# The last head's output weights on 16 partitions, in a load of two times 8

## Chip, cores, metric

The kernel runs on one core of one Trainium2 chip. The metric is the device time of one execution in microseconds (us). Three runs of the kernel before took 1311.43, 1311.44 and 1311.72 us; the median is 1311.44.

## What is computed

One decoding step of a block with grouped-query attention and a gate. There are 2 batch rows, 32 query heads over 8 key/value heads, 32768 cached positions, head size 128, model size 512, all in float32. Cut to what matters:

```
xn  = layernorm(x)                                  # (2, 1, 512)
q   = xn @ wq                                       # 32 heads of 128
s   = softmax(q k^T / sqrt(128)) v                  # per head, 32768 keys and values
att = concat(s) @ wo                                # wo is (4096, 512)
g   = silu(relu(xn @ w1 + b1)^2 @ w2 + b2)
out = x + att * g
```

The caches are 2 x 8 x 32768 x 128 numbers each, 537 MB together; wq and wo are 8.4 MB each.

## The kernel before

**Stages.** The work goes over 16 pairs s of a key/value head and a batch row (`hkv, b = divmod(s, 2)`). For each, the keys come in four quarters: VectorE transposes them in 32 x 32 blocks (L248), TensorE makes the scores with q as the stationary side (L253), a softmax follows (`softmax`, `probs`), and TensorE sums the values with the probabilities (L316, `values`). When a pair's values are summed, its four heads are turned into columns of `oT` (L323 to L328). After the last pair the output projection runs (`project`, L395 to L404), the result is multiplied by the gate and added to x (L406, L407), and two small stores end the kernel (L409).

**Transfers.** Nearly all loads are issued by SP, in the order of the list `loads` (L136 to L141). An entry with an event is issued when that event is given (`give`), and waits on SP until its buffer has been read. Keys go to three slots of 4 MB (`kslots`), values to `vbuf` of 8 MB; the value load before the last goes to the first two key slots. The output weights come last: `load_wo(i)`, i = 0 to 3, each a group of 8 heads or 1024 rows of wo, 2 MB. Groups 0 and 1 lie in slot 2, groups 2 and 3 in slot 0, which is free when TensorE has read the first half of the value load before the last.

**The layout of wo.** A group is loaded as `(p j) e -> p j e`: partition p holds the eight rows 8p to 8p+7 of the group, 16 KB without a break. For the projection, row 8p+j must meet the attention output of the same number, so the columns of `oT` (partition = place in the head, one column per head) are spread to `oW[p, i, j, b]`. That happens when the second head pair of a group is done (`hkv % 2 == 1`, L329 to L336): VectorE multiplies the 8 columns by the selector `sele` (L332), TensorE multiplies that by `selj` (L335), ScalarE copies the 8 columns (L336). `project` then makes one matmul for each j and each of 4 column groups of 128 outputs; `oW` has 32 columns for the batch, of which 2 are used. A float32 matmul stands in the profile as two instructions.

**The last group** comes in four pieces of j (`PIECES`, L33, L128, L129): 4, 2, 1 and 1 of the eight rows of every partition, that is 1 MB, 512 KB and twice 256 KB. The projection takes groups 0, 1, 2 and then the pieces in this order.

The order of instructions on an engine is made by the framework's scheduler from the program's order; waits between engines are semaphores that it sets.

Of the kernel before, what the change touches and what calls it, by code (L numbers as in the profile page):

```python
# [9 lines left out]
F32 = mybir.dt.float32  # L10
AF = mybir.ActivationFunctionType
ALU = mybir.AluOpType
AX = mybir.AxisListType

P = 128
# [14 lines left out]
TS = (1, 0, 2, 3)  # L30
NT = 4
HALF = 64 * 128
PIECES = ((0, 4), (4, 6), (6, 7), (7, 8))  # L33


@with_exitstack
def gqa_decode_kernel(ctx: ExitStack, tc: tile.TileContext, x, kc, vc, wq, wo, w1, b1, w2, b2, out):
    nc = tc.nc
    B, _, D = x.shape
    _, HKV, SK, DH = kc.shape  # L40
    HQ = wq.shape[1] // DH
# [7 lines left out]
    DE = D // NG  # L49
    WG = 8  # L50
    NWG = HQ // WG
# [6 lines left out]
    const = ctx.enter_context(tc.tile_pool(name="const", bufs=1))  # L58
    ktpool = ctx.enter_context(tc.tile_pool(name="ktpool", bufs=8))
    work = ctx.enter_context(tc.tile_pool(name="work", bufs=2))  # L60
# [3 lines left out]
    def misc(name):  # L64
        return pms.tile([P, 512], F32, tag="ms", name=name)
# [51 lines left out]
        return t.rearrange("p (j e) -> p j e", j=FJ)  # L117


    def load_wo(i):  # L120
        if i % 2 == 0:
            wide[i // 2] = kslots[:, 2 - i].rearrange("p (i j e) -> p i j e", i=2, j=WG)
        t = wide[i // 2][:, i % 2]
        src = wo[i * WG * P:(i + 1) * WG * P, :].rearrange("(p j) e -> p j e", p=P)
        if i < NWG - 1:
            nc.sync.dma_start(t, src)
        else:
            for j0, j1 in PIECES:  # L128
                nc.sync.dma_start(t[:, j0:j1, :], src[:, j0:j1, :])  # L129
        return t  # L130

    wide = {}
    NK, NV = NS * NT, NS * NCH
    kslots = const.tile([P, 3, HALF], F32, name="kslots")
    vbuf = const.tile([P, 2 * HALF], F32, name="vbuf")
    loads = [(None, load_wq, 0), (None, load_half, 0), (None, load_half, 1), (("q", 0), load_w1, 0),  # L136
             (("s", 0), load_half, 2), (None, load_half, 3), (("q", 0), load_w2, 0)]
    for m in range(2, NV):
        loads += [(("s", 2 * m - 2), load_k, m), (("v", m - 3) if m > 2 else ("w", 1), load_v, m - 2)]
    loads += [(("s", NK - 2), load_v, NV - 2), (("v", NV - 3), load_v, NV - 1)]  # L140
    loads += [(("s", NK - 1), load_wo, 0), (("s", NK - 1), load_wo, 1), (("v", NV - 2), load_wo, 2), (("v", NV - 2), load_wo, 3)]  # L141
    past = {None}
    done = [0]
# [7 lines left out]
    def take(f, a):  # L151
        return tiles.pop((f, a))

    def give(*event):
        past.add(event)
        issue()
# [4 lines left out]
    ident = const.tile([P, P], F32, name="ident")  # L161
# [12 lines left out]
    selj = const.tile([P, WG], F32, name="selj")  # L174
    nc.vector.tensor_reduce(selj, ident.rearrange("p (e j) -> p j e", j=WG), axis=AX.X, op=ALU.add)
    sele = const.tile([P, P // WG], F32, name="sele")
    nc.vector.tensor_reduce(sele, ident.rearrange("p (e j) -> p e j", j=WG), axis=AX.X, op=ALU.add)
    oT = const.tile([P, HQ, B], F32, name="oT")
    oW = const.tile([P, NWG, WG, 32], F32, name="oW")
    nc.gpsimd.memset(oW, 0.0)  # L180
    sc = [pone.tile([P, 512], F32, tag=f"sc{i}", name=f"sc{i}") for i in range(NT)]
    o_ps = [pone.tile([P, 512], F32, tag=f"o{i}", name=f"o_ps{i}") for i in range(2)]
    for t in o_ps:
# [16 lines left out]
    t_ps = misc("xnT_ps")  # L200
# [6 lines left out]
    for d in range(ND):  # L207
        for f in range(2):
            for g in range(NG):
                cc = f * NG + g  # L210
                nc.tensor.matmul(sc[f][32 * g:32 * g + 32, :], xnT[:, d, 0:32], wqt[:, d, cc * 512:(cc + 1) * 512],  # L211
                                 start=(d == 0), stop=(d == ND - 1))
    give("q", 0)
    qT = const.tile([P, B, HKV, REP, 4], F32, name="qT")
    for f in range(2):
        for h in range(REP):
# [3 lines left out]
            t_ps = misc(f"qT_ps{f}_{h}")  # L220
# [87 lines left out]
    def values(n):  # L308
        s, k = divmod(n, NCH)
        vt = take(load_v, n)  # L310
        o = o_ps[s % 2]
        for c in range(2):
            for i in range(NO // 4):
                for g in range(NG):
                    lo = (c * NG + g) * NO + 4 * i
                    nc.tensor.matmul(o[32 * g:32 * g + 16, :], pT[s][:, k, g, c, 4 * i:4 * i + 4, :].rearrange("p o h -> p (o h)"),  # L316
                                     vt[:, lo:lo + 4, :].rearrange("p o d -> p (o d)"),
                                     start=(k + c + i == 0), stop=(k == NCH - 1 and c == 1 and i == NO // 4 - 1))
        give("v", n)
        if k == NCH - 1:  # L320
            hkv, b = divmod(s, B)
            o_sb = work.tile([P, 512], F32, tag="o_sb", bufs=1, name=f"o_sb{s}")
            nc.scalar.copy(o_sb, o)  # L323
            t_ps = misc(f"oT_ps{s}")
            r4 = rs.pop(s)
            for i in range(4):
                nc.tensor.matmul(t_ps[:, :REP], o_sb[:, i * DH:(i + 1) * DH], r4[:, i, :], start=(i == 0), stop=(i == 3))  # L327
            nc.vector.tensor_copy(oT[:, hkv * REP:(hkv + 1) * REP, b], t_ps[:, :REP])  # L328
            if hkv % 2 == 1:  # L329
                i = hkv // 2  # L330
                m = work.tile([P, WG, P // WG], F32, tag="om", bufs=1, name=f"om{s}")
                nc.vector.tensor_mul(m, oT[:, i * WG:(i + 1) * WG, b:b + 1].to_broadcast([P, WG, P // WG]),  # L332
                                     sele[:, None, :].to_broadcast([P, WG, P // WG]))
                t_ps = misc(f"oW_ps{s}")
                nc.tensor.matmul(t_ps[:, :WG], m.rearrange("p h e -> p (h e)"), selj, start=True, stop=True)  # L335
                nc.scalar.copy(oW[:, i, :, b], t_ps[:, :WG])  # L336


    hT, gate = first[:, 3, :FJ * 32].rearrange("p (j b) -> p j b", j=FJ), const.tile([P, DE], F32, name="gate")
# [33 lines left out]
    for n in range(NK):  # L373
        s, i = divmod(n, NT)
        if i == 0:
            set_q(s)
        scores(n)
        if n == 1:
            mlp_up()
        if n == 3:  # L380
            mlp_down()
        if i == 3:
            softmax(s)
        if n >= 5 and n % 2 == 1:
            values((n - 5) // 2)
        if i == 3:
            probs(s)
    values(NV - 2)
    values(NV - 1)


    a_ps = sc[0]
    wot = [take(load_wo, i) for i in range(NWG)]

    def project(i, j0, j1):  # L395
        for j in range(j0, j1):
            for g in range(NG):
                nc.tensor.matmul(a_ps[32 * g:32 * g + 32, :DE], oW[:, i, j, :], wot[i][:, j, g * DE:(g + 1) * DE],
                                 start=(i == 0 and j == 0), stop=(i == NWG - 1 and j == WG - 1))

    for i in range(NWG - 1):
        project(i, 0, WG)
    for j0, j1 in PIECES:
        project(NWG - 1, j0, j1)  # L404
    asb = work.tile([P, DE], F32, tag="e", bufs=1, name="a_sb")
    nc.vector.tensor_mul(asb, gate, a_ps[:, :DE])  # L406
    nc.vector.tensor_add(xe, asb, xe)  # L407
# [25 lines left out]
```

## Time and profile before

| what | before |
|---|---|
| time, median of 3 runs | 1311.44 us |
| the profiled execution, its own time | 1311.62 us |
| its span, first to last instruction | 1309.6 us |
| TensorE matmul (PE), weight load (PEld) busy | 885.4, 251.1 us |
| VectorE (DVE), ScalarE (ACT), GpSimd (POOL) busy | 648.8, 88.3, 15.1 us |
| moved by DMA | 561.74 MB, mean 429 GB/s |
| packets of queue q1 (SP's), of q8 (instructions) | 10952, 38 |

The profile is of one execution. Busy times are shares of the span in which an engine worked; DMA share is the mean busy share of the core's 16 DMA engines, PEclk the granted clock of TensorE, 1.00 being full speed. A line of the timeline gives start, duration, engine, line of the kernel, operation, tiles and count; brackets hold the idle time before it and what ended that. The trace also holds one record for each DMA packet (start, duration, size, queue) and one for each completion mark. A load that uses 16 DMA engines ends with 16 marks; who waits for the load waits for all of them.

### The profile page before, as it was taken

Reading aid. Unit: us, or ns where it says so; the run is one execution under the profiler, and the core shown is the slowest. Engines: PE = TensorE matmul, PEld = TensorE weight load, DVE = VectorE, ACT = ScalarE, POOL = GpSimd, SP = SyncE. Lnnn points to the kernel's source line nnn. Section 1 sums busy time; section 2 is a strip of 40 time slices with the busy share of each in tenths; the row PEclk is TensorE's granted clock in tenths of the full one; section 3 lists DMA queues with packets and bytes.
Section 4 is the critical chain, followed back from the end, with each engine's and each line's share of the span. In section 5 each row is a group of like instructions: output and inputs, shape, how many; then the busy total and the mean of one; then the engine's idle time right before and its main releaser. Section 6 shows DMA issues by size and latency. Waiting matters only on the chain.

```text
span 1309.6 us, 11506 instructions
## 1 busy us (share of the span) xinstructions
PE 885.4 (68%) x4926; PEld 251.1 (19%) x4926; DVE 648.8 (50%) x742; ACT 88.3 (7%) x237; POOL 15.1 (1%) x76
## 2 busy tenths in 40 slices
PE   3867675658757567775657766566875756776575
PEld 1222121112212111121212211111221211112123
DVE  2855654435555344655435565443655534465410
ACT  0010010101001010000101001010000101000010
POOL 0000000000000000000000000000000000000000
PEclk9988877888878788877789978778987878888788
DMA  9999999999999999999999999999999999999997
GB/s 403 433 441 439 424 439 423 441 433 431 435 427 435 435 427 443 423 439 428 437 429 431 435 427 443 419 443 429 435 435 427 439 427 437 435 425 441 421 441 303
DMA packets 11040, 561.74 MB, mean 429 GB/s; under 512 B 1239, under 2 KB 1259, under 8 KB 1646
## 3 DMA queue, kind: packets, MB, share of 16 engines
q1 hardware_dynamic: 10952, 561.00, 99.2%
q8 instruction: 38, 0.62, 0.2%
q14 instruction: 12, 0.10, 0.0%
q10 hardware_dynamic: 38, 0.02, 0.0%
HBM read 561.01 MB, written 0.00 MB: 428 GB/s over the span
## 4 chain that ended last, share of the span: by engine, by line
DMA 74%; DVE 18%; issue 5%; PE 2%; SPq 0%; DVEq 0%
DMA kslots<-in_A_k_cache 68%; DVE kt L248 18%; DMA kslots<-in_A_wo 2%; DMA kslots<-in_A_v_cache 2%; DMA vbuf<-in_A_wq 2%; PE sc L211 1%; PE o_ps L316 0%; PE h_ps L347 0%; SPq L129 0%; DVE qr L218 0%; DVEq L248 0%; PE qT_ps L222 0%; PE sc L253 0%; DVE h L354 0%; DVE first L355 0%
## 5 line engine op out<-in xcount | busy, mean ns | idle before, releaser
L253 PE MATMUL sc<-kt,qz 128*32 128x512 f32 x2048 | 578.4, 671 | 330.6 <-DVE kt L248 309.0
L248 DVE STREAM_TRANSPOSE kt<-kslots 128x1024 f32<-128x1024 f32 x512 | 580.7, 1205 | 350.9 <-DMA kslots<-in_A_k_cache 350.9
L253 PEld LDWEIGHTS sc<-kt,qz 128*32 128x32 f32 x2048 | 112.0, 115 | 783.1 <-DVE kt L248 580.7
L316 PE MATMUL o_ps<-vbuf,pT 128*16 128x512 f32 x1984 | 228.8, 597 | 11.0 <-DMA vbuf<-in_A_v_cache 11.0
L316 PEld LDWEIGHTS o_ps<-vbuf,pT 128*16 128x16 f32 x1984 | 76.7, 97 | 139.9 <-issue 119.6
L275 ACT ACTIVATE p<-sc,nm 128x512 f32<-128x512 f32 x32 | 23.3, 746 | 991.0 <-DVE nm L271 991.0
L328 DVE COPY oT<-oT_ps 128x4 f32<-128x4 f32 x16 | 2.6, 162 | 121.5 <-PE oT_ps L327 121.5
L258 DVE TENSOR_REDUCE rm<-sc 128x1 f32<-128x512 f32 x32 | 22.1, 691 | 63.9 <-PE sc L253 63.9
L294 ACT COPY pT<-pT_ps 64x256 f32<-64x256 f32 x128 | 46.8, 366 | 19.7 <-PE pT_ps L290 18.2
L300 DVE RECIPROCAL r<-l_ps 128x4 f32<-128x4 f32 x16 | 2.9, 182 | 46.2 <-PE l_ps L298 46.2
L231 POOL COPY qz<-qT 32x16 f32<-32x16 f32 x64 | 12.7, 198 | 1077.4 <-PE sc L253 1042.5
L327 PE MATMUL oT_ps<-rs,o_sb 128*128 128x4 f32 x128 | 16.9, 255 | 11.5 <-ACT o_sb L323 11.4
L290 PE MATMUL pT_ps<-ident,p 128*128 128x128 f32 x128 | 20.2, 309 | 2.9 <-ACT p L275 2.9
L327 PEld LDWEIGHTS oT_ps<-rs,o_sb 128*128 128x128 f32 x128 | 15.5, 191 | 25.6 <-ACT o_sb L323 25.6
L298 PE MATMUL l_ps<-lh,ones 128*128 128x4 f32 x32 | 8.2, 327 | 17.6 <-ACT pT L294 17.6
L290 PEld LDWEIGHTS pT_ps<-ident,p 128*128 128x128 f32 x128 | 17.4, 169 | 3.1 <-ACT p L275 3.1
L323 ACT COPY o_sb<-o_ps 128x512 f32<-128x512 f32 x16 | 9.4, 585 | 100.1 <-PE o_ps L316 100.1
L278 DVE TENSOR_REDUCE l<-l 128x1 f32<-128x2 f32 x16 | 2.5, 155 | 26.9 <-ACT p L275 26.9
L264 PE MATMUL mx_ps<-ident,rm 128*128 128x128 f32 x16 | 5.2, 323 | 14.6 <-DVE rm L262 14.6
L202 PE MATMUL xnT_ps<-ident,xn 128*128 128x128 f32 x4 | 1.1, 428 | 20.4 <-DVE xn L198 20.4
L316 PE MATMUL o_ps<-kslots,pT 128*16 128x512 f32 x64 | 8.4, 682 | 4.2 <-DMA kslots<-in_A_v_cache 4.2
L298 PEld LDWEIGHTS l_ps<-lh,ones 128*128 128x128 f32 x32 | 6.8, 266 | 22.0 <-ACT pT L294 22.0
(68 smaller groups left out, 116.2 us busy)
## 6 DMA issues: line engine op xcount, KB each, us to landing
kslots<-in_A_k_cache SPq DMA_DIRECT2D x4, 4096.0 KB, 20.8
vbuf<-in_B_w SPq DMA_DIRECT2D x2, 3584.0 KB
kslots<-in_A_wo SPq DMA_DIRECT2D x3, 2048.0 KB
kslots<-in_A_wo SPq DMA_DIRECT2D x1, 1024.0 KB
kslots<-in_A_wo SPq DMA_DIRECT2D x1, 512.0 KB
kslots<-in_A_wo SPq DMA_DIRECT2D x2, 256.0 KB, 31.3
vbuf<-in_A_v_cache SPq DMA_DIRECT2D x31, 31.0
kslots<-in_A_k_cache SPq DMA_DIRECT2D x30
```

Source lines behind the costliest of these rows:

```text
L211: nc.tensor.matmul(sc[f][32 * g:32 * g + 32, :], xnT[:, d, 0:32], wqt[:, d, cc * 512:(cc + 1) * 512], start=(d == 0), stop=(d == ND - 1))
L231: nc.gpsimd.tensor_copy(qz[s % 2][32 * a:32 * a + 32, 16:].rearrange("p (e y) -> p e y", e=4)[:, :, a * REP:(a + 1) * REP], qT[32 * a:32 * ...
L248: nc.vector.transpose(r.rearrange("p e o w -> p o e w"), kt[:, g * NO:(g + 1) * NO, e0 * 32:(e0 + 2) * 32].rearrange("p o (e w) -> p o e w ...
L253: nc.tensor.matmul(bank[32 * g:32 * g + 32, :], qz[s % 2][:, lo + 32 * (e0 + e):lo + 32 * (e0 + e) + 32], kts[g][:, e].rearrange("p o w -> ...
L258: nc.vector.tensor_reduce(rm[s][:, u:u + 1], bank, axis=AX.X, op=ALU.max)
L275: nc.scalar.activation(p[:, :, :, u], sc[2 * (s % 2) + u].rearrange("p (o w) -> p o w", w=32), AF.Exp, bias=nm, scale=SCALE, accum_out=l2[ ...
L290: nc.tensor.transpose(t_ps[:, j * P:(j + 1) * P], p[:, o:o + 2].rearrange("p o w u -> p (o w u)"), ident)
L294: nc.scalar.copy(sb[64 * a:64 * a + 64].rearrange("p k g c (i j o) h -> p i o j (g c) k h", i=2, o=2)[:, i, o], v[:, :, :, :, a])
L298: nc.tensor.matmul(t_ps[:, :REP], ones, lh, start=True, stop=True)
L316: nc.tensor.matmul(o[32 * g:32 * g + 16, :], pT[s][:, k, g, c, 4 * i:4 * i + 4, :].rearrange("p o h -> p (o h)"), vt[:, lo:lo + 4, :].rear ...
L323: nc.scalar.copy(o_sb, o)
L327: nc.tensor.matmul(t_ps[:, :REP], o_sb[:, i * DH:(i + 1) * DH], r4[:, i, :], start=(i == 0), stop=(i == 3))
```

## The change

The last group is no longer one block of 1024 rows. Its last head (128 rows of wo, 256 KB) is loaded by itself to 16 partitions (`few`, in slot 1), 8 rows or 16 KB on each. The source is written `(n y j) e -> y n (j e)` with y = 2, so that partition 8y+n holds the rows 8(2n+y) to 8(2n+y)+7 of the head. This load is issued ahead of the others. The seven heads before it come in three pieces of 4, 2 and 1 heads; each piece is now a block of its own (`(p j) e -> p j e` with j = 4, 2, 1), where a partition's rows lie together in wo.

The spread to `oW` changes accordingly for this group: one multiply and matmul for the four heads, one for the two, a copy for the single head, and one for the last head into `oF`, 16 partitions by 8 rows. Two selector pairs (`sels`) are made at the start. `oW` has 16 batch columns instead of 32. The projection takes groups 0 to 2, then the four heads, the eight rows of `few`, the two heads and the one.

```diff
-PIECES = ((0, 4), (4, 6), (6, 7), (7, 8))
+PIECES = ((0, 4, 0), (4, 2, 4), (6, 1, 6))
...
-            for j0, j1 in PIECES:
-                nc.sync.dma_start(t[:, j0:j1, :], src[:, j0:j1, :])
+            base = (HQ - 1) * P
+            nc.sync.dma_start(few, wo[base:base + P, :].rearrange("(n y j) e -> y n (j e)", y=2, j=WG))
+            for h0, nh, j0 in PIECES:
+                base = (i * WG + h0) * P
+                nc.sync.dma_start(t[:, j0:j0 + nh, :], wo[base:base + nh * P, :].rearrange("(p j) e -> p j e", p=P))
...
+few = kslots[0:16, 1, 0:WG * D]
...
+    for nh in (4, 2):
+        sels[nh] = const.tile([P, P // nh + nh], F32, name=f"sel_{nh}")
+        nc.vector.tensor_reduce(sels[nh][:, 0:P // nh], ident.rearrange("p (e j) -> p e j", j=nh), axis=AX.X, op=ALU.add)
+        nc.vector.tensor_reduce(sels[nh][:, P // nh:], ident.rearrange("p (e j) -> p j e", j=nh), axis=AX.X, op=ALU.add)
-    oW = const.tile([P, NWG, WG, 32], F32, name="oW")
+    oW = const.tile([P, NWG, WG, 16], F32, name="oW")
+    oF = const.tile([16, WG, 16], F32, name="oF")
...
+                def spread(h0, nh, se, sj, x0):
+                    m = work.tile([P, P], F32, tag="om", bufs=1, name=f"om{s}_{h0}")
+                    nc.vector.tensor_mul(m.rearrange("p (h e) -> p h e", h=nh),
+                                         oT[:, h0:h0 + nh, b:b + 1].to_broadcast([P, nh, P // nh]),
+                                         se[:, None, :].to_broadcast([P, nh, P // nh]))
+                    nc.tensor.matmul(t_ps[:, x0:x0 + nh], m, sj, start=True, stop=True)
...
+                    for h0, nh, j0 in PIECES[:-1]:
+                        spread(i * WG + h0, nh, sels[nh][:, 0:P // nh], sels[nh][:, P // nh:], j0)
+                    h0, _, x0 = PIECES[-1]
+                    nc.scalar.copy(oW[:, i, 0:x0, b], t_ps[:, :x0])
+                    nc.vector.tensor_copy(oW[:, i, x0, b:b + 1], oT[:, i * WG + h0, b:b + 1])
+                    m = work.tile([P, P], F32, tag="om", bufs=1, name=f"om{s}_few")
+                    nc.vector.tensor_mul(m[:, 0:16].rearrange("p (y n) -> p y n", y=2),
+                                         oT[:, HQ - 1:HQ, b:b + 1].to_broadcast([P, 2, 8]),
+                                         sele.rearrange("p (n y) -> p y n", y=2))
+                    nc.tensor.matmul(t_ps[0:16, 8:8 + WG], m[:, 0:16], selj, start=True, stop=True)
+                    nc.scalar.copy(oF[:, :, b], t_ps[0:16, 8:8 + WG])
...
-    for j0, j1 in PIECES:
-        project(NWG - 1, j0, j1)
+    project(oW[:, NWG - 1], wot[NWG - 1], j0, j0 + nh)
+    project(oF, few.rearrange("p (j e) -> p j e", j=WG), 0, WG)
+    for h0, nh, j0 in PIECES[1:]:
+        project(oW[:, NWG - 1], wot[NWG - 1], j0, j0 + nh, stop=(j0 + nh == WG - 1))
```

More of the change, by code (lines that the diff above doesn't have):

```diff
@@ L177, in gqa_decode_kernel @@
     nc.vector.tensor_reduce(sele, ident.rearrange("p (e j) -> p e j", j=WG), axis=AX.X, op=ALU.add)
+    sels = {}
+    for nh in (4, 2):
+        sels[nh] = const.tile([P, P // nh + nh], F32, name=f"sel_{nh}")
+        nc.vector.tensor_reduce(sels[nh][:, 0:P // nh], ident.rearrange("p (e j) -> p e j", j=nh), axis=AX.X, op=ALU.add)
+        nc.vector.tensor_reduce(sels[nh][:, P // nh:], ident.rearrange("p (e j) -> p j e", j=nh), axis=AX.X, op=ALU.add)
     oT = const.tile([P, HQ, B], F32, name="oT")
-    oW = const.tile([P, NWG, WG, 32], F32, name="oW")
+    oW = const.tile([P, NWG, WG, 16], F32, name="oW")
     nc.gpsimd.memset(oW, 0.0)
+    oF = const.tile([16, WG, 16], F32, name="oF")
+    nc.gpsimd.memset(oF, 0.0)
     sc = [pone.tile([P, 512], F32, tag=f"sc{i}", name=f"sc{i}") for i in range(NT)]
@@ L330, in values @@
                 i = hkv // 2
-                m = work.tile([P, WG, P // WG], F32, tag="om", bufs=1, name=f"om{s}")
-                nc.vector.tensor_mul(m, oT[:, i * WG:(i + 1) * WG, b:b + 1].to_broadcast([P, WG, P // WG]),
-                                     sele[:, None, :].to_broadcast([P, WG, P // WG]))
                 t_ps = misc(f"oW_ps{s}")
-                nc.tensor.matmul(t_ps[:, :WG], m.rearrange("p h e -> p (h e)"), selj, start=True, stop=True)
-                nc.scalar.copy(oW[:, i, :, b], t_ps[:, :WG])
+                def spread(h0, nh, se, sj, x0):
[4 more added lines that the diff above has]
+                    nc.tensor.matmul(t_ps[:, x0:x0 + nh], m, sj, start=True, stop=True)
+                if i < NWG - 1:
+                    spread(i * WG, WG, sele, selj, 0)
+                    nc.scalar.copy(oW[:, i, :, b], t_ps[:, :WG])
+                else:
+                    for h0, nh, j0 in PIECES[:-1]:
[9 more added lines that the diff above has]
+                    nc.scalar.copy(oF[:, :, b], t_ps[0:16, 8:8 + WG])
     hT, gate = first[:, 3, :FJ * 32].rearrange("p (j b) -> p j b", j=FJ), const.tile([P, DE], F32, name="gate")
@@ L393, in gqa_decode_kernel, with project @@
     wot = [take(load_wo, i) for i in range(NWG)]
-    def project(i, j0, j1):
+    def project(ow, wt, j0, j1, start=False, stop=False):
         for j in range(j0, j1):
             for g in range(NG):
-                nc.tensor.matmul(a_ps[32 * g:32 * g + 32, :DE], oW[:, i, j, :], wot[i][:, j, g * DE:(g + 1) * DE],
-                                 start=(i == 0 and j == 0), stop=(i == NWG - 1 and j == WG - 1))
+                nc.tensor.matmul(a_ps[32 * g:32 * g + 16, :DE], ow[:, j, :], wt[:, j, g * DE:(g + 1) * DE],
+                                 start=start and j == j0, stop=stop and j == j1 - 1)
     for i in range(NWG - 1):
-        project(i, 0, WG)
-    for j0, j1 in PIECES:
-        project(NWG - 1, j0, j1)
+        project(oW[:, i], wot[i], 0, WG, start=(i == 0))
+    h0, nh, j0 = PIECES[0]
+    project(oW[:, NWG - 1], wot[NWG - 1], j0, j0 + nh)
+    project(oF, few.rearrange("p (j e) -> p j e", j=WG), 0, WG)
+    for h0, nh, j0 in PIECES[1:]:
+        project(oW[:, NWG - 1], wot[NWG - 1], j0, j0 + nh, stop=(j0 + nh == WG - 1))
     asb = work.tile([P, DE], F32, tag="e", bufs=1, name="a_sb")
```

## The prediction

> **What bounds the kernel now.** I read the page first: 561 MB at 429 GB/s, DMA share 9 tenths in 39 of 40 slices. Engine work matters only where it delays an issue until the queue runs dry, or after the last byte. So I went to the end of the chain of waits (start us, us, what):
>
> ```profile
> 1274.05 31.46 DMA kslots<-in_A_wo
> 1305.50 0.04 issue
> 1305.55 0.47 PE sc L398 x8
> 1306.02 0.02 issue
> 1306.04 0.30 DVE a_sb L406
> ```
>
> The last transfer is issued at 1274.05 and lands at 1305.50: it stands in a full queue. Then come 8 matmul instructions, the gate (L406, L407) and the store. The change works in these last ten microseconds, so I cut them into stretches (the last two columns are DMA share and GB/s, PEclk before them):
>
> ```profile
> 1296.00:1298.00 2.00, 2.00 (x42) 1.76 (x45) 0.46 (x2) 0.18 (x1) 0.00 (x0) 1.00 0.98 393
> 1298.00:1299.50 1.50, 1.50 (x64) 1.50 (x60) 0.00 (x0) 0.00 (x0) 0.00 (x0) 1.00 0.67 273
> 1299.50:1302.00 2.50, 2.23 (x83) 1.96 (x77) 0.00 (x0) 0.00 (x0) 0.00 (x0) 1.00 0.52 217
> 1302.00:1303.50 1.50, 0.90 (x36) 0.66 (x31) 0.00 (x0) 0.00 (x0) 0.00 (x0) 1.00 0.56 220
> 1303.50:1305.00 1.50, 1.42 (x47) 0.88 (x40) 0.00 (x0) 0.00 (x0) 0.00 (x0) 1.00 0.35 134
> ```
>
> The DMA share falls to 0.52 six microseconds before the end, and to 0.35: most of the 16 DMA engines are done while a few still carry their part. The trace's records of completion marks say which. The last piece's 16 marks land at 1298.32 to 1299.31 (seven engines), 1303.64 to 1303.85 (three) and 1305.25 to 1305.50 (six). An engine's packets follow each other without a gap, so I chained them through the run. The 16 KB instruction packets (38 on the page) go in turn to the same eight engines; one hit puts an engine about 1.5 us further behind (2.19 to 3.74 us, at 309 us), and nothing catches up.
>
> The third view is TensorE's own time:
>
> ```profile
> 1296.56 0.85 PE L398 MATMUL sc<-kslots,oW 128*32 128x128 f32 x22
> 1297.35 0.39 PE L335 MATMUL oW_ps<-selj,om 128*128 128x8 f32 x2
> 1297.66 2.61 PE L398 MATMUL sc<-kslots,oW 128*32 128x128 f32 x88
> 1300.55 1.95 PE L398 MATMUL sc<-kslots,oW 128*32 128x128 f32 x64 [0.28 <-DMA kslots<-in_A_wo]
> 1303.10 2.23 PE L398 MATMUL sc<-kslots,oW 128*32 128x128 f32 x56 [0.60 <-DMA kslots<-in_A_wo]
> 1305.55 0.42 PE L398 MATMUL sc<-kslots,oW 128*32 128x128 f32 x8 [0.21 <-DMA kslots<-in_A_wo]
> ```
>
> TensorE waits for DMA three times, but only 0.28, 0.60 and 0.21 us. Eight instructions are one row index j (4 column groups, 2 passes each); one pass of four starts every 0.109 us in the record, so a j costs 0.218 us and a group of 8 heads 1.74 us.
>
> **The DMA side.** Bytes stay the same. Today the last group gives each engine 8 rows of 8 KB (0.306 us each), 4 KB (0.156) and twice 2 KB (0.080). After, the second 2 KB piece (0.64 us per engine) is gone, and 16 rows of 16 KB (0.611 each in the records of the groups before) stand ahead of the others. On how many engines? The nearest rows are small loads whose two sides have one outer count: two rows of x ran on two engines, four rows of b1 on four, one row of b2 on one, 128 partitions on all 16. The new load has 16 outer steps at SBUF and 2 at wo. The bounds are 16 engines with one row each and two with eight; I take two, since the side with 2 steps is shaped like the x load.
>
> [...]
>
> Then two engines get 8 x 0.611 = 4.89 us more and the other fourteen 0.64 us less, all told. Which two decides everything. The x load and the four loads of xe, two rows each, sit in the same two chains at 7.6 to 27 us; followed to the end, both are among the seven early engines. Their 8 KB pieces land today at 1296.3 and 1296.74; 4.89 later is 1301.63, before the late six deliver theirs at 1302.97. So the first piece still completes at 1302.97, the half-size one at 1304.23, the last (now the third) at 1304.87 instead of 1305.50. The few rows themselves land by 1296.74 - 2.45 + 4.89 = 1299.2.
>
> The load also waits until TensorE has read the second half of the value slot (L316 ends at 1274.9, against 1271.58 for the first half), and the three pieces queue behind it on SP: about 1277 instead of 1274 for the last issue. The early engines reach this group only at about 1292.8; cover 15 us, cost nothing.
>
> **The TensorE side.** The last group becomes 4 + 8 + 2 + 1 = 15 j instead of 8, since the last head now has 8 rows on 16 partitions. Order written in the kernel: four heads, the few rows, two heads, one head. All 15 come after 1302.97, in one run without the waits that stand there today: 120 instructions, 30 passes, 3.27 us from the landing of the first piece. For tiles with few rows the trace has one row, next to the full one:
>
> ```profile
> L365 PE MATMUL y_ps<-vbuf,first x112: 272/273/297, 81.7 to 85.5; 128*32 128x128 f32 x112
> L361 PE MATMUL y_ps<-first,ones x8: 267/280/292, 40.6 to 40.8; 1*32 1x128 f32 x8
> ```
>
> One row takes as long as 128 (280 against 273 ns), and its second pass starts 0.133 us after the first, as L398's does after a stop. So no gain by few rows. Halving the stationary columns of oW (32 to 16) I cost at nothing: the weight loads lie beside the matmuls (PEld busy 1.69 us in the 1.95 of group 2). The bound is the difference of the two weight loads in the last 70 us, 109 ns for L398's 32 columns and 104 for L316's 16: 0.15 us in 30 passes. Going from tiles of 128 rows to 32 and back has no row of its own here; the nearest is L327 to L398 (full array to column tiles), where the next start comes after 0.18 instead of 0.11 us. I take 0.07 each, between 0 and 0.25.
>
> [...]
>
> Sum: landing 1302.97, start 0.13 later as today (1303.10), 30 passes of which 28 up to the start of the last j (3.05), 0.02 for the first pass, 0.14 for two switches, 0.47 from there to the gate: 1306.78. Today 1306.04. **The end moves by +0.75 us**: the DMAs win 0.63, and TensorE takes the bound and more.
>
> **Does TensorE reach 1303.0 on time?** The spread of the oT columns (L332 to L336) becomes three multiplies, three matmuls and two copies with one buffer for the product, so each multiply waits for the matmul before. In the built order the first has its inputs early; the others stand between instructions of group 0. Today: multiply 1296.86, matmul 1297.35, copy 1297.77. After: second matmul about 1297.4, third multiply once that has read (1297.84), third matmul 1298.2, rest of group 0 until 1299.0, groups 1 and 2 (1.74 each) until 1302.5. Today it is 1302.3 (1300.55 + 1.74), and then TensorE stops for 0.60 us; 0.4 us of that cover is left. Beyond it each further 0.1 us counts in full. For the head before, the same extra steps fall at 1258, where TensorE later idles 4.2 us ahead of the value load (1266.55).
>
> **The start.** Four more selector sums (0.28 us apart) join this queue:
>
> ```profile
> 19.41 0.28 DVE L177 TENSOR_REDUCE sele<-ident 128x16 f32<-128x128 f32 x1
> 19.61 0.16 DVE L197 RECIPROCAL st<-st 128x1 f32<-128x1 f32 x1
> ...
> 21.57 0.69 DVE L203 COPY first<-xnT_ps 128x512 f32<-128x512 f32 x1 [1.28 <-PE xnT_ps L202]
> ```
>
> The copy ends about 23.4 instead of 22.3 and passes the landing of wq, so the query projection (23.00) starts some 0.5 us later, as does the issue that waits for it. The packets run without a gap past 70.95, when the first waiting key load is issued, to 77.3, so 6 us of queue hide it; uncovered it would be 0.5 us.
>
> **Forecast.** 1311.62 (1309.6 of span, 2.0 around it) + 0.75 = 1312.4 against the profiled execution. That run is 0.18 above the median of the runs shown, 1311.44, so against the median: **1312.2**. 0.2% is 2.6 us, about what a measurement of this kernel tells from no change; this is within it.
>
> **Rivals.**
> - *Sixteen engines share the load, one row each* (it does not do what it says): every engine gets 0.61 before the first piece, which completes at 1303.58; the same TensorE run follows: +1.36, 1312.8. For: 16 partitions at SBUF. Against: 2 steps at wo. 0.12.
> - *TensorE hides the seven extra j*: the end follows the last piece, 0.63 earlier, 1310.8. It needs the few rows' 64 instructions in about 0.4 us, not 1.74; the L361 row speaks against. 0.08.
> - *The two engines are late ones*, the other side: their first piece would land at 1302.97 + 4.89 = 1307.9 (middle three: 1306.0), and TensorE's run starts from there: +5.6 (+3.8), 1317.0 (1315.2). It begins to cost when an engine's first piece lands today after 1298.08, and passes 0.2% at 1299.95; my two stand at 1296.3 and 1296.74. Against it: the chains, unambiguous for one, with one exchange of names to be resolved for the other. 0.08.
> - Faster by over 0.2% has no mechanism; 0.02 for what I don't see.
>
> Forecast 0.70. Faster by over 0.2%: 0.02; within: 0.70 + 0.12 + 0.08 = 0.90; slower: 0.08. The range goes from the hidden case, 1310.8, to the sixteen-engine case with both switches at 0.25, 1313.2.
>
> **What will show it.** Right: the few rows' load as 16 packets of 16 KB in two chains; last marks at about 1304.9; no stop of TensorE between 1303.1 and 1306.6; L442 starts near 1306.8. Wrong: a wait for DMA ahead of the last eight matmuls, marks after 1305.5, or passes of the few rows closer than 0.109 us.

## The result and the profile after

The changed kernel takes 1316.55 us (median of six runs, 1315.83 to 1318.19) against 1311.43 for the kernel before: ratio 1.0039, 95% interval [1.0029, 1.005]. It is slower by 5.1 us, more than the forecast (1312.2) and its range (to 1313.2) allowed. The span of the profiled execution is 1314.8 us, before 1309.6.

The end of the chain of waits (start us, us, what), to be held against 1274.05, 1305.55 and 1306.04 in the lines of before:

```profile
1276.37 29.49 DMA kslots<-in_A_wo
1305.90 5.25 PE sc L431 x120
```

The wait for the last piece is gone, as forecast: all 120 matmul instructions of the last group are one run. But that run starts at 1305.90 and not at 1303.10, and it lasts until the gate at 1311.17. TensorE's own time shows the same (start, duration, line, tiles; brackets hold the idle time before):

```profile
1298.90 2.55 PE L431 MATMUL sc<-kslots,oW 128*16 128x128 f32 x80
1302.45 1.94 PE L431 MATMUL sc<-kslots,oW 128*16 128x128 f32 x64 [1.00 <-DMA kslots<-in_A_wo]
1305.90 1.07 PE L431 MATMUL sc<-kslots,oW 128*16 128x128 f32 x32 [1.51 <-DMA kslots<-in_A_wo]
1306.90 2.79 PE L431 MATMUL sc<-kslots,oF 16*16 16x128 f32 x64
1309.62 1.48 PE L431 MATMUL sc<-kslots,oW 128*16 128x128 f32 x24
```

Where 0.28, 0.60 and 0.21 us stood, there are now 1.00 us before group 2 and 1.51 before the first piece. And there is a second difference: 64 instructions of the few rows take 2.79 us where 64 of a full group take 1.94. The same run in four stretches (the last three columns are PEclk, DMA share and GB/s):

```profile
1305.90:1306.90 1.00, 1.00 (x32) 0.79 (x33) 0.00 (x0) 0.00 (x0) 0.00 (x0) 1.00 0.11 43
1306.90:1308.20 1.30, 1.30 (x47) 1.25 (x47) 0.00 (x0) 0.00 (x0) 0.00 (x0) 0.85 0.08 20
1308.20:1309.60 1.40, 1.40 (x28) 0.90 (x20) 0.00 (x0) 0.00 (x0) 0.00 (x0) 0.50 0.00 0
1309.60:1311.10 1.50, 1.50 (x28) 0.83 (x24) 0.00 (x0) 0.00 (x0) 0.00 (x0) 0.50 0.00 0
```

The granted clock falls from 1.00 to 0.50 in the middle of the run (at 1307.82 by the clock's records, which change only at multiples of 3.41 us in all twelve traces); from there a pass starts every 0.213 us instead of 0.109. Not the 16-row tiles are slow: up to 1307.8 their passes came every 0.109 us too.

The marks of the transfers explain the late start. The few rows' load has two marks, so two engines carried it, as predicted. One landed at 1298.66 (predicted: by 1299.2), the other at **1303.70**. The trace's packet records of that second engine, and of one of the late six in the same time (start, end, ns, bytes):

```
second engine with few rows            a late engine, end of group 2
1293.602 1294.275  673 16384
1294.271 1295.465 1194 16384
1295.462 1296.687 1225 16384
1296.683 1297.883 1200 16384
1297.880 1298.833  953 16384
1298.829 1300.069 1240 16384           1298.697 1299.885 1188 16384
1300.065 1301.343 1278 16384           1299.882 1301.161 1279 16384
1301.340 1302.619 1279 16384           then 8 KB packets of 0.65
```

A 16 KB packet takes 1.2 us instead of 0.611, and another engine is slow in step. The few rows of the second engine took 9.02 us (1293.60 to 1302.62), not 4.89; its first-piece mark came at 1305.86, the last of 16. The late engine's came at 1305.42. Of 312 packets of 16 KB from 1285 to 1305 us only ten took over 0.8 us: nine of these, and one beside an instruction packet, as there is one in the kernel before. Up to 1298.8 the engine slow in step is one that had already come to the smaller pieces: one chain's 8 KB packets took 0.61 to 0.63 us instead of 0.309 and its 4 KB packets 0.28 to 0.32 instead of 0.159 (1294.17 to 1298.77).

The two parts add up: first piece 1305.86 instead of 1302.97, 2.89; run of TensorE from there to the gate 5.31 us instead of 3.07, 2.24, of which 0.74 was forecast and 1.50 was not; most of this is the clock (1.3 by e5_warm below). Together 5.13, the gate's delay (1306.04 to 1311.17).

### The profile page after: what moved, and what is told of

Its sections match the earlier page's. It is cut to its first block, busy times and chain, and to the rows that moved or that the text cites. A ratio compares the mean times of both kernels' runs of the same rounds, so it can differ in the third digit from the quotient of the medians.

```text
span 1314.8 us, 11650 instructions
## 1 busy us (share of the span) xinstructions
PE 889.7 (68%) x4990; PEld 252.3 (19%) x4990; DVE 650.8 (49%) x752; ACT 88.6 (7%) x239; POOL 14.8 (1%) x77
## 4 chain that ended last, share of the span: by engine, by line
DMA 73%; DVE 19%; issue 5%; PE 2%; DVEq 0%; SPq 0%; ACTq 0%
DMA kslots<-in_A_k_cache 68%; DVE kt L263 18%; DMA kslots<-in_A_wo 2%; DMA kslots<-in_A_v_cache 2%; DMA first<-in_A_x 1%; PE sc L226 1%; PE o_ps L331 1%; PE sc L431 0%; PE h_ps L380 0%; DVE qr L233 0%; DVEq L263 0%; PE qT_ps L237 0%; PE sc L268 0%; PE xnT_ps L217 0%; DVE h L387 0%
## 5 line engine op out<-in xcount | busy, mean ns | idle before, releaser
L431 PE MATMUL sc<-kslots,oW 128*16 128x128 f32 x248 | 9.1, 287 | 2.5 <-DMA kslots<-in_A_wo 2.5
```

Source lines behind the costliest of these rows:

```text
L431: nc.tensor.matmul(a_ps[32 * g:32 * g + 16, :DE], ow[:, j, :], wt[:, j, g * DE:(g + 1) * DE], start=start and j == j0, stop=stop and j == ...
```

## The experiments

Theory A: two DMA engines that write the same small group of SBUF partitions share one way into it, and each then takes twice as long (1.2 us for a packet of 16 KB instead of 0.611). A load of 128 partitions gives each of 16 engines eight packets, one for each partition (128 packets of 8 KB and 16 marks for the first piece of before); the load of few rows sends an engine to partitions that another one is filling. No trace names the partitions of an engine, so it must show in runs; where an expectation below says which engine fills a place, that is the theory's assumption. Rival B: two engines are simply slow at eight packets each, or the form of the load is at fault, wherever the rows go.

### e1_own: the same rows, to partitions 0 to 7 and 32 to 39

In the edits of this section, three dots stand for further lines: the place of `few` and `oF`, the spread to `oF`, the body of a function.

```diff
-            nc.sync.dma_start(few, wo[base:base + P, :].rearrange("(n y j) e -> y n (j e)", y=2, j=WG))
+            for q in range(2):
+                nc.sync.dma_start(few[32 * q:32 * q + 8], wo[base + 64 * q:base + 64 * q + 64, :].rearrange("(n y j) e -> y n (j e)", y=2, j=WG))
...
```

> The rows of the last head go in two loads of 2 x 4 partitions, to partitions 0-7 and 32-39, instead of one of 2 x 8 to partitions 0-15; source rows, two DMA engines, eight packets of 16 KB each and everything else as in the changed kernel. Theory A (shared way into SBUF): in the changed kernel the second of the two engines writes partitions 8-15, which other engines also write in every load over 128 partitions, and two engines that write the same few partitions at once each get half. [...] A expects packets of about 0.61 us in both chains (1.2 to 1.28 in one of them in the changed kernel), the first piece complete near 1303.0 instead of 1305.86, TensorE's run of 3.8 us to the gate at full clock, and about 1312.2 us in all. Rival B (the load itself: two engines on one 256 KB stretch of wo, or a load on few engines): the packets of 1.2 us stay, about 1316.5.

Measured: 1312.65 us, ratio 1.0009 [0.9999, 1.0018]. Of 316 packets of 16 KB from 1285 to 1305 us one took over 0.8 us (changed kernel: 10 of 312). The few rows landed at 1298.32 and 1299.04, the first piece at 1303.09, the last at 1304.96. TensorE:

```profile
1303.13 1.07 PE L435 MATMUL sc<-kslots,oW 128*16 128x128 f32 x32 [0.24 <-DMA kslots<-in_A_wo]
1304.13 0.93 PE L435 MATMUL sc<-kslots,oF 40*16 40x128 f32 x25
1305.36 1.28 PE L435 MATMUL sc<-kslots,oF 40*16 40x128 f32 x39 [0.30 <-issue]
1306.57 0.85 PE L435 MATMUL sc<-kslots,oW 128*16 128x128 f32 x24
```

The landings are those of the forecast within 0.12 us (1302.97 and 1304.87), with the partitions alone changed; the time is 0.45 above its 1312.2. The clock stayed at 1.00 too, with a wait of 0.24 us and a stop of 0.30 where the changed kernel had waits of 1.00 and 1.51. The gate stood at 1307.49, 0.3 of it a stop of TensorE for which the profile names no releaser.

### e7_foreign: the same two loads, eight partitions higher

```diff
-                nc.sync.dma_start(few[32 * q:32 * q + 8], wo[base + 64 * q:base + 64 * q + 64, :].rearrange("(n y j) e -> y n (j e)", y=2, j=WG))
+                nc.sync.dma_start(few[32 * q + 8:32 * q + 16], wo[base + 64 * q:base + 64 * q + 64, :].rearrange("(n y j) e -> y n (j e)", y=2, j=WG))
...
```

> As e1_own, two loads of 2 x 4 partitions, but to partitions 8-15 and 40-47 instead of 0-7 and 32-39; the spread has eight more zero columns. Theory A (two DMA engines that write the same small group of partitions slow each other): both engines that carry the few rows now write partitions that two other engines write at the same time; their 16 KB packets take about 1.2 us instead of 0.61 for as long as the others write there, the few rows land at about 1303 to 1304, the first piece is complete at 1305.8 to 1306.5, and the time is 1316 to 1317.2. Rival B (the two loads' form is what helped in e1_own, not the partitions): as e1_own, 1312.65, packets at 0.61 to 0.65.

Measured: 1318.95 us, ratio 1.0055 [1.004, 1.007], 6.3 us above e1_own. Of that, 5.0 us are the landing of the first piece; the run from there to the gate is 5.67 us against 4.40, since TensorE's clock fell to half in a wait of 4.15 us (1304.14 to 1310.97). The few rows landed at 1302.90 and 1304.09 as A had it, the first piece at 1308.09, later than it had. The reason is in the windows, e1_own first, then e7_foreign:

```profile
1294.00:1298.00 4.00, 3.88 (x62) 2.65 (x54) 0.52 (x3) 0.58 (x1) 0.00 (x0) 1.00 0.96 400
1298.00:1302.00 4.00, 3.99 (x141) 3.72 (x145) 0.24 (x2) 0.49 (x3) 0.00 (x0) 1.00 0.68 285
```

```profile
1294.00:1298.00 4.00, 3.87 (x61) 2.49 (x53) 0.52 (x3) 0.59 (x1) 0.00 (x0) 1.00 1.02 211
1298.00:1302.00 4.00, 3.33 (x98) 2.69 (x96) 0.23 (x3) 0.49 (x3) 0.00 (x0) 1.00 0.95 198
```

The DMA share is full and the rate is half. 78 of 310 packets of 16 KB took over 0.8 us. From 1294.7 to 1298 no packet of SP's loads escaped: all 26 of 16 KB that started then took 1.23 to 1.28 us, and all of 8 KB and 4 KB about twice their 0.309 and 0.159 (in e1_own one packet of 146 was slow). That the partitions decide is shown: nothing in the loads differs but eight partitions. That *only* the colliding engines suffer, as A said, fell here.

### e2_far, e8_own64, e3_sixteen: other places

e2_far puts the load of the changed kernel on partitions 64 to 79, e8_own64 the loads of e1_own on 64 to 71 and 96 to 103; e3_sixteen makes the load one of 16 outer steps on both sides, one row for each engine:

```diff
-    few = kslots[0:16, 1, 0:WG * D]
+    few = kslots[64:80, 1, 0:WG * D]
...
```

```diff
-    few = kslots[0:40, 1, 0:WG * D]
+    few = kslots[64:104, 1, 0:WG * D]
...
```

```diff
-            nc.sync.dma_start(few, wo[base:base + P, :].rearrange("(n y j) e -> y n (j e)", y=2, j=WG))
+            nc.sync.dma_start(few, wo[base:base + P, :].rearrange("(n j) e -> n (j e)", j=WG))
...
```

> The same load of 2 x 8 partitions goes to partitions 64-79 instead of 0-15; nothing else differs from the changed kernel. Theory A: now neither engine writes partitions of its own; four other engines do that in the loads over 128 partitions. Both chains should show packets of about 1.2 us as long as those four are busy, and so should parts of those four chains; first piece complete at 1305 or later, 1315 to 1319 us. Rival B: destination does not matter, one slow chain as in the changed kernel, 1316.5.

> As e1_own, two loads of 2 x 4 partitions, but to partitions 64-71 and 96-103. Theory A, narrow: two engines and two others that own these partitions slow each other, the other twelve do not: 1316 to 1317.2, as e7_foreign. Rival C, wide: partitions 64 and up slow nearly all engines' packets to 1.1 to 1.3 us, as in e2_far: about 1318.3. Rival B (the form of the two loads): 1312.65.

> The same 16 rows of 16 KB in a load with one outer count of 16 on both sides, so that 16 DMA engines take one row each; the selector is changed to the new order of rows, the rest is as in the changed kernel. Plain counting (no shared way in): each engine 0.61 us more ahead of the first piece, which completes at 1303.6; gate at 1307.4, about 1312.8. Theory A: sixteen engines write into 16 partitions that four engines serve in the big loads; packets of those that meet take 1.2 us or more instead of 0.61, so up to some 2 us per engine, first piece at 1303.6 to 1305, 1312.8 to 1315. Rival B: if a load on few engines is the trouble, packets are 0.61 and the time 1312.8.

Measured: 1318.29 us (1.0051 [1.0036, 1.0066]), 1317.26 (1.0045 [1.0028, 1.0062]) and 1315.94 (1.0038 [1.0026, 1.005]). The window 1294 to 1298 of e2_far, then of e8_own64:

```profile
1294.00:1298.00 4.00, 3.88 (x61) 2.55 (x53) 0.52 (x3) 0.58 (x1) 0.00 (x0) 1.00 1.02 220
```

```profile
1294.00:1298.00 4.00, 3.87 (x77) 2.97 (x73) 0.76 (x5) 0.76 (x2) 0.00 (x0) 1.00 1.01 212
```

76 and 68 slow packets: wide, like e7_foreign, and again every packet that started from 1294.7 to 1298 was slow. Since e7_foreign writes partitions 8 to 15 and 40 to 47, it is not the partitions from 64 up that make it wide. e8_own64 against e1_own says that the two-loads form is no help by itself, so rival B falls. In e3_sixteen 32 of 309 were slow, in two short stretches: all 13 packets of 16 KB that started from 1292.76 to 1293.28 (0.94 to 1.68 us), then none from 1294.78 to 1298.84. Its first piece came at 1305.84, later than A had it (1305 at most), and TensorE waited again:

```profile
1302.71 1.94 PE L429 MATMUL sc<-kslots,oW 128*16 128x128 f32 x64 [0.72 <-DMA kslots<-in_A_wo]
1305.88 1.07 PE L429 MATMUL sc<-kslots,oW 128*16 128x128 f32 x32 [1.23 <-DMA kslots<-in_A_wo]
```

Sixteen engines with a row each would have cost 0.61 us by the prediction's rival; they write the 16 partitions 0 to 15, and the first piece is 2.87 late.

### e9_onesided, e10_oneport: narrow or wide

The load of e9_onesided, then that of e10_oneport, against e1_own's:

```diff
-            for q in range(2):
-                nc.sync.dma_start(few[32 * q:32 * q + 8], wo[base + 64 * q:base + 64 * q + 64, :].rearrange("(n y j) e -> y n (j e)", y=2, j=WG))
+            for q in range(4):
+                nc.sync.dma_start(few[q:q + 97:32], wo[base + 32 * q:base + 32 * q + 32, :].rearrange("(n y j) e -> y n (j e)", y=2, j=WG))
...
```

```diff
-            for q in range(2):
-                nc.sync.dma_start(few[32 * q:32 * q + 8], wo[base + 64 * q:base + 64 * q + 64, :].rearrange("(n y j) e -> y n (j e)", y=2, j=WG))
+            for q in range(8):
+                nc.sync.dma_start(few[8 + q:41 + q:32], wo[base + 16 * q:base + 16 * q + 16, :].rearrange("(y j) e -> y (j e)", j=WG))
...
```

> As e1_own, but the few rows in four loads of two times two partitions, 32 apart: one of the two DMA engines writes partitions 0-3 and 32-35, which it writes in every load; the other 64-67 and 96-99, which a third engine writes. The few rows' matmuls and spread take all 128 partitions, zeros elsewhere. The question is what makes the slowdown narrow in the changed kernel (10 packets of 16 KB over 0.8 us from 1285 to 1305) and wide in e7_foreign and e8_own64 (78 and 68, 198 to 211 GB/s at a DMA share of 0.95 to 1.02). Theory 1 (one collision slows its two engines alone, two collisions at once slow all): here 8 to 20 packets over 0.8 us, 350 GB/s or more from 1294 to 1298, the second engine's 8 packets at about 1.2, first piece complete at about 1306, 1316 to 1317. Theory 2 (one collision of this kind, wholly with one other engine, is enough): 60 or more packets over 0.8 us, about 210 GB/s from 1294 to 1298, 1317 to 1319.

> As e7_foreign (partitions 8-15 and 40-47), but in eight loads of two partitions 32 apart, so that the two DMA engines with the few rows write the same group of partitions at the same time (8-11 and 40-43, then 12-15 and 44-47), together with the one engine that writes it in every load. Theory 1 (all are slowed when two groups are contended at once): only three engines are slow at a time, their packets at about 1.8 us, 24 to 40 packets over 0.8 us, 300 GB/s or more from 1294 to 1298. Theory 2 (all are slowed when both engines of the small load are out of their own group, whichever group it is): 60 or more packets over 0.8 us, about 210 GB/s from 1294 to 1298. The time is 1317 to 1320 by both.

e9_onesided: 1314.7 us, ratio 1.0026 [1.0015, 1.0038]; six slow packets of 16 KB, five of them 1.18 to 1.27 us and one beside an instruction packet. Its window:

```profile
1294.00:1298.00 4.00, 3.88 (x56) 2.27 (x52) 0.17 (x2) 0.58 (x1) 0.00 (x0) 1.00 0.95 359
```

Narrow, as theory 1 has it, but with fewer slow packets than its 8 to 20. The other engine's smaller packets (8, 4 and 2 KB) took about twice their time up to 1299.85 and then ended, and the second engine's last slow packet ended at 1300.70. So the first piece came at 1304.83, not at 1306; TensorE waited 0.97 us, its clock stayed at 1.00, and the time is below the 1316 to 1317 expected. The profiled execution is the fastest of seven (1313.67 to 1316.34), so in others the collision may have cost more.

e10_oneport: 1321.75 us, ratio 1.0078 [1.0063, 1.0093], but the time says little, since SP held back: the eight small loads took it from 1276.22 to 1304.28 to issue, and the pieces went out only then. The packets do speak. From 1294.6 to 1297.1, two chains ran at 1.19 to 1.20 us a packet, and when a third joined, three at once (the trace's records, start, end, ns):

```
1299.149 1300.944 1795
1299.431 1301.232 1801
1299.493 1301.299 1806
1300.946 1302.699 1753
```

1.2 us for two, 1.8 for three: one group of partitions takes a 16 KB packet in every 0.6 us, whoever sends it. Only 18 of 307 packets were over 0.8 us, fewer than the 24 to 40 of theory 1 and far from the 60 of theory 2. From 1294.7 to 1298, where every packet of e7_foreign was slow, 7 of 50 were, and the rest ran at 0.61. The GB/s (254 from 1294 to 1298, below the 300 of theory 1) are of no use, since some engines had nothing queued: the DMA share was 0.69. With that reserve theory 2 falls; with a full queue this case was not run.

The runs suggest how large a group is. By the edits one engine wrote 0 to 3 and 32 to 35 in e1_own, the other 4 to 7 and 36 to 39 (one slow packet of 316); in e9_onesided the second, on 64 to 67 and 96 to 99, met one other engine (six slow packets); in e10_oneport both met one, on places 32 apart (1.8 us a packet). That makes a group of four partitions and the four 32 above them, an estimate from these three runs. With it, one group contended at a time (changed kernel, e9_onesided, e10_oneport) leaves 6 to 18 packets of 16 KB slow; two at once (e2_far, e7_foreign, e8_own64) 68 to 78. All six runs fit, and so does the first stretch of e3_sixteen, where the estimate has four groups contended. No trace shows how many were contended in the last four, nor what holds back the engines that have no part in a collision.

### e5_warm: the clock

```diff
+    def fill(n):      # matmuls into sc[1], which nobody reads
...
     for i in range(NWG - 1):
+        if i > 0:
+            fill(4 if i == 1 else 7)
```

> The changed kernel with 44 row indices (352 instructions) of filler matmuls into a bank that nobody reads, placed ahead of the second and the third group of eight heads, so that TensorE is at work up to the landing of the first piece; nothing else is changed and the output does not use them. Theory: the last 1.5 us of the 5.1 us come from TensorE's clock, which the records show halved from 1307.82 on after the two waits of 1.0 and 1.5 us. With the fillers the clock stays at 1.00 until the gate, the run from the first piece's landing (1305.86) to the gate takes about 3.8 us instead of 5.3, and the time is about 1315.0. Rival: the halving comes from something else (a limit on power or a fixed beat) and stays, or the slow packets are what counts: 1316.5.

The fillers are fewer than that text says: 4 + 7 = 11 row indices, 88 instructions, which the program has behind the second and the third group. In the trace they run between 1298.60 and 1303.1.

Measured: 1315.53 us, ratio 1.0031 [1.0019, 1.0043]. The first piece landed at 1305.95, as late as in the changed kernel, but the clock held:

```profile
1306.00:1307.30 1.30, 1.30 (x48) 1.09 (x48) 0.00 (x0) 0.00 (x0) 0.00 (x0) 1.00 0.15 47
1307.30:1308.60 1.30, 1.30 (x56) 1.30 (x52) 0.00 (x0) 0.00 (x0) 0.00 (x0) 1.00 0.00 2
1308.60:1309.90 1.30, 1.30 (x38) 0.71 (x28) 0.00 (x0) 0.00 (x0) 0.00 (x0) 1.00 0.00 0
```

The gate came 4.02 us after the landing (1309.97), not 5.31. So the halving came with the waits, and it cost 1.3 us (1.0 by the medians, whose intervals overlap). A limit on power does not fit, since TensorE did more work here, nor does a fixed beat: the clock stood at 1.00 for 23.9 us, in the changed kernel for 17.1. The forecast of 3.81 for this run was 0.2 short.

### e4_blocks and e6_own_first: the rest of the change, and the order

e4_blocks drops the few rows: the last head is a fourth piece of one head, everything else of the change stays.

```diff
-PIECES = ((0, 4, 0), (4, 2, 4), (6, 1, 6))
+PIECES = ((0, 4, 0), (4, 2, 4), (6, 1, 6), (7, 1, 7))
...
```

> The last head goes back to 128 partitions as a fourth piece of one row; what stays of the change are the pieces as blocks of their own, the spread in parts, the 16 batch columns and the selectors at the start. All theories that put the loss into the 16-partition load expect the time of before, 1311.4 within 0.5 us: pieces of the same sizes land at the same times, and TensorE has 8 row indices again. Rival C (the spread or the blocks cost): over 1312.5.

Measured: 1311.65 us, ratio 1.0001 [0.9991, 1.001]; last piece 1306.01, gate 1306.53, and one run without a stop:

```profile
1299.19 7.27 PE L421 MATMUL sc<-kslots,oW 128*16 128x128 f32 x218
```

Selectors, spread chain, block layout and 16 columns cost nothing that can be measured. The whole loss belongs to the few rows (their load, their own step of the spread, their seven further row indices).

e6_own_first takes the loads of e1_own (not shown again), and the few rows' matmuls ahead of the four heads:

```diff
+    project(oF, few.rearrange("p (j e) -> p j e", j=WG), 0, WG)
     project(oW[:, NWG - 1], wot[NWG - 1], j0, j0 + nh)
-    project(oF, few.rearrange("p (j e) -> p j e", j=WG), 0, WG)
```

> The last head's load as in e1_own (two loads of 2 x 4 partitions, 0-7 and 32-39), and TensorE takes the few rows' eight row indices ahead of the four heads of the first piece, in the wait for that piece. Theory: the few rows land at about 1299.0, TensorE comes free at about 1302.3, the few rows end at 1304.1, the four heads at 1305.0 without a wait, so only 7 of 15 row indices follow... the last piece lands at about 1304.96, the end of TensorE's run is not later than 1305.9, the gate at about 1306.4, and the time is 1311.4 to 1311.9 (before 1311.5). Rival: the run is bound by its 30 passes in whatever order they stand (1312.65, as e1_own).

Measured: 1312.53 us, ratio 1.0008 [0.9999, 1.0018]: no better than e1_own. The third line has the reason:

```profile
1298.73 3.88 PE L435 MATMUL sc<-kslots,oW 128*16 128x128 f32 x130
1302.53 1.81 PE L435 MATMUL sc<-kslots,oF 40*16 40x128 f32 x57
1305.42 0.41 PE L435 MATMUL sc<-kslots,oF 40*16 40x128 f32 x7 [1.08 <-issue]
1305.75 1.72 PE L435 MATMUL sc<-kslots,oW 128*16 128x128 f32 x56
```

TensorE stands for 1.08 us with all its data there; without that the gate (1307.54) would be at 1306.46, as expected. In e1_own the stop came ahead of the same instruction, 63 before the end (39 + 24 there, 7 + 56 here), and ended at 1305.36, here at 1305.42. A 16 KB instruction packet ran at 1302.80 to 1303.82 there and at 1302.91 to 1304.00 here. e5_warm has a third such stop (1.12 us, no releaser, to 1305.16, such a packet at 1302.66 to 1303.76). That points to TensorE waiting for its instructions; no run moved the packets, so it is not shown.

## Why the prediction was wrong, point by point

- **The failed step** is "two engines get 8 x 0.611 = 4.89 us more", and with it "so the first piece still completes at 1302.97". The price was taken from loads over 128 partitions, eight packets for each of 16 engines. Which partitions the 16 rows go to was not looked at. The second engine took 9.02 us; that is 4.13 more, and its first 8 KB packet, at 0.634, another 0.32. Without both it would have completed at 1301.41 (predicted: up to 1301.63), so 1.56 was covered by the late engines (1302.97), and the landing was 2.89 late. e1_own and e7_foreign show it: same rows, same engines, 1312.65 and 1318.95.
- **A second step failed behind it**: 3.27 us of TensorE after the landing were priced at full clock, with no case for a clock that falls after a wait. The run took 5.31 us where 3.81 was priced, 1.50 more; against e5_warm 1.3 of that is the clock. Waits of 1.00 and 1.51 us went ahead of it (0.72 and 1.23 in e3_sixteen, where the clock fell at 1308.92); a single one of 1.12 in e5_warm, 1.08 in e6_own_first and 0.97 in e9_onesided did not bring it on before the gate. Whether the longer wait or the sum of two counts is not shown; no idle stretch of TensorE between the clock's rise at 1290.75 and its fall was longer than the 1.51.
- Right: two engines, both early ones; the first one's landing (1298.66 against 1299.2); 0.109 us a pass whatever the rows; the fifteen row indices as one run, with nothing gained from the earlier last piece. The price of that run was 0.2 short (e5_warm): the start after a change of tile form came 0.222 us after the pass before, not 0.109, so 0.11 each where 0.07 stood. That is 0.08 of it; where the rest lies is not shown.
- Right: the hidden parts. The last issue was at 1276.37 (forecast about 1277); the query projection started at 22.95, as before (23.00), so even the 0.5 us there did not come; e4_blocks puts the sum of the rest at 1.0001.
- Of the rivals none was it. The one on the other side had a late transfer as its mechanism and a time near the result (1315.2 to 1317.0), but through the wrong engines: the two were early, as the forecast said. The sixteen-engine rival's price, 1312.8, would have been wrong by the same step: measured 1315.94.

## What to carry to other kernels

A small load that runs on few DMA engines must be priced by where it writes as well as by how many engines carry it: if another load is filling those partitions at the time, try the same load on others and count the slow packets (here one of 316 on 0 to 7 and 32 to 39, 78 of 310 eight partitions higher, and 6.3 us between the two times). A load placed ahead of the final pieces delays them by the slowest engine: here one engine's 4.13 us more put the first piece 2.89 late, whatever time the others had to spare. Where waits like those of the changed kernel (1.00 and 1.51 us) or of e3_sixteen (0.72 and 1.23) stand ahead of the last matmuls, price these at half clock as a second case; single waits of about one microsecond (0.97 to 1.12) did no harm here.

## What the runs showed of the hardware

One group of partitions took a 16 KB packet in every 0.6 us, with one, two or three engines writing (0.61, 1.2, 1.8 us a packet). In e2_far, e7_foreign and e8_own64 every packet of SP's loads that started from 1294.7 to 1298 took about twice its time (211 to 220 GB/s from 1294 to 1298, at a DMA share of 1.01 to 1.02, against 400 at 0.96 in e1_own). TensorE's clock halved at 1307.82, two microseconds into its work and after waits of 1.00 and 1.51 us.
